# Convolution and SoLU layer: y's transposes and copies issued from a list, each behind a transpose of p, from tile 17 on

## Chip, cores and metric

The kernel runs on one core of a Trainium2 chip. The metric is the device time of one execution in microseconds; lower is better. Before the change three runs took 1172.75, 1173.3 and 1176.29 us, median 1173.3 us.

## What is computed

x has 8 sequences of 4160 positions with 192 features. The first step is a causal convolution over 7 positions with softmax weights for each of 8 heads; the second is a feed-forward layer of width 1024 with the SoLU activation and a layer norm. Cut to what matters:

```python
def _attn_ref(x, weight):                      # weight: 8 heads x 7 taps
    ...
    w = w / (np.sum(w, axis=-1, keepdims=True) + 1e-09)
    ...
    out = np.einsum('hk,bskhg->bshg', w, x_unf)
    return out.reshape(B, S, D).astype(np.float32)

def _moe_ref(x, w_in, w_out, g_ln):            # 33280 x 192, 192 x 1024, 1024 x 192
    h = x @ w_in
    h_max = np.max(h, axis=-1, keepdims=True)
    e = np.exp(h - h_max)
    sm = e / (np.sum(e, axis=-1, keepdims=True) + 1e-09)
    solu = h * sm
    mu = np.mean(solu, axis=-1, keepdims=True)
    var = np.mean((solu - mu) ** 2, axis=-1, keepdims=True)
    ln = (solu - mu) / np.sqrt(var + 1e-06) * g_ln
    return (ln @ w_out).astype(np.float32)
```

## The kernel before

The 33280 rows are 260 **tiles** of 128 rows (index i). The convolution works on **chunks**: 17 pieces of a sequence, from chunk 2 on half a sequence (2080 rows) each, so 16 or 17 tiles. The first tiles of chunks 2 to 16 are 16, 32, 48, 65, 81, 97, 113, 130, 146, 162, 178, 195, 211, 227 and 243.

**A chunk's way.** `load` (L139) brings x into buffers xr, four pieces a chunk. `sum_squares` (L174) takes the largest magnitude of half a piece on VectorE (L181, into xa); from all of them `scale_steps` makes the chunk's scale (L203 and after). GpSimd splits x into two float16 parts, xs (L236, L240, L243; `halve_steps`). `product` (L258) convolves on TensorE (L281, into pc); ScalarE writes y's upper part (`upper`, L313) and VectorE its lower (`lower`, L322) into y16. A chunk's y16 has two parts, the first ten windows of 112 rows and the other nine, each with three blocks of 128 columns (0: upper, 2: lower, 1: the rest of both). `turn` (L351) transposes one block of one part into yT by a DMA on SyncE's queue (L352), in the order of blocks 1, 0, 2; `double` (L361) copies half of block 1 to y2 (L365). `open` (L327) gets yT and y2 for a chunk and copies the rows that the chunk before left over.

**A tile's way.** `emit_rows` (L730) multiplies blocks 0, 0, 2, 1 of yT with w_in in eight matmuls (L736, into ph), in this order; `emit_third` (L756) adds the lower part of w_in with half arrays (L759) from yT's block 1 or from y2. VectorE takes the maximum (`emit_max`, L790), ScalarE the exponential (L797), VectorE the product (L807), ScalarE the upper half p (L815), GpSimd the lower half (`emit_lo`, L827), and behind it SyncE issues the transpose of p into pT (L829). Five tiles later `emit_out` (L831) multiplies pT with w_out (L843, into po); VectorE adds it up into raw (`emit_evac`, L850), later the row's factor is applied (L917, L921) and two tiles' rows are stored (L930).

**What sets the order.** Everything is in the order in which the program is written. From tile 8 on `three_steps` (L1276) issues a **triplet** of tiles a, b, c; its first tile i is 8, 11, 14, and so on. All DMAs stand in SyncE's one queue, in order, and a transpose of p waits there for its p. `chores` (L964) spreads a chunk's loads, convolutions, transposes (`"turn"`), copies (`"double"`) and sums over the tiles of the chunk before it, or of one two or three chunks before. In a triplet with i ≥ 16 (`start` is false), x's loads come at the beginning; opening and transposes that are due come at the end, behind the transpose of p of c (`openings`, L1334); copies that are due wait in `doubles` until the next triplet, behind the transpose of p of its a. Triplets with i < 16 are ordered otherwise.

Of the kernel before, what the change touches and what calls it, by code (L numbers as in the profile page):

```python
# [19 lines left out]
def kernel(  # L20
# [346 lines left out]
    chunks = [Chunk(ch) for ch in range(NCH)]  # L367
# [184 lines left out]
    for e, bank in enumerate(banks):  # L552
        for q in range(2 * per):
# [4 lines left out]
                start=q == 0, stop=q == 2 * per - 1,  # L558
# [267 lines left out]
    def emit_lo(t, eng):  # L826
        eng.tensor_tensor(t.p16[:, :, 1, :], t.halves, t.p16[:, :, 0, :], ALU.subtract)  # L827
        t.pT = sp.tile([P, 2 * NFC, P], F16, name=f"pT_{t.i}", tag="pT", bufs=4)
        nc.sync.dma_start_transpose(t.pT, t.p16.rearrange("p n a f -> p (n a f)"))  # L829
# [113 lines left out]
    tiles, lefts, left = [], [], 0  # L943
# [153 lines left out]

    PAIRED = FIRST // P
    assert spans[0][2] == PAIRED * P and PAIRED == 8 and (NT - PAIRED) % 3 == 0
    early, doubles, squares, late = [], [], [], []  # L1100

    def prepare(i):
        t = tiles[i]
# [15 lines left out]
    def numerators(t):  # L1119
        emit_mul(t)  # L1120
        emit_hi(t)
# [142 lines left out]
    def others(ts):  # L1264

        work = {}
        for q in ts:
            for what, items in chores(q.ch, q.k, q.n).items():
                work.setdefault(what, []).extend(items)
        return work  # L1270

    def loads(work):
        for c, j in work.get("load", []):
            c.load(j)

    def three_steps(i):  # L1276
# [4 lines left out]
        work = others(ts)  # L1281
# [13 lines left out]
        urgent = i == PAIRED + 3  # L1295

        start = i < 2 * PAIRED
        if not start:
            loads(work)
        got = {}  # L1300

        def add(n):
            for c, h in added[n]:
                sum_up(c, h, i + 2)
# [16 lines left out]
        def at(n):  # L1321
            return [q for q in got.get(n, []) if q]

        def uppers(n):
            for k, pc, hg in at(n):
                if not k.scaled and k.exact:
                    run_chain(20)
                k.upper(pc, *hg)

        def lowers(n):  # L1330
            for k, pc, hg in at(n):
                k.lower(pc, *hg)

        def openings():  # L1334
            for k in work.get("open", []):
                k.open(lefts[k.ch], chunks[k.ch - 1])
            for k, piece in work.get("turn", []):
                k.turn(*piece)
# [40 lines left out]
            doubles.clear()  # L1379
        numerators(a)  # L1380
        emit_lo(a, pool)
        if i == PAIRED:
            uppers(2)
            late[:] = after
# [17 lines left out]
        emit_square(a)  # L1402
        numerators(b)
        emit_lo(b, pool)
        if not start:
            lowers(2)
        for f in rest:
            f()
# [27 lines left out]
        if urgent:  # L1436
            for k, q in work["double"]:
                k.double(*q)
        else:
            openings()  # L1440
            doubles.extend(work.get("double", []))
        if i == NT - 6:
            ready(b)
        queue.run(3.8 if i < 20 else 2.0)
# [2 lines left out]
    def ready(t):  # L1447
        emit_z(t)
        emit_root(t)
# [58 lines left out]
    for i in range(PAIRED, NT - 3, 3):  # L1508
        three_steps(i)
# [28 lines left out]
```

## Time and profile before

| | |
|---|---|
| median of three runs | 1173.3 us (1172.75 to 1176.29) |
| the profiled execution, whole | 1174.77 us |
| its span, first to last instruction | 1173.1 us |
| TensorE matmuls busy | 97% of the span |
| DMA on SyncE's queue | 1.0 busy share of 16 engines in most of 40 slices |
| granted TensorE clock | 1.00 in every slice |

How to read the profile: PE is TensorE's matmuls, PEld its weight loads, DVE VectorE, ACT ScalarE, POOL GpSimd. SPq is SyncE, which only issues DMAs; a row's duration there is the time until SyncE goes on, not that of the transfer. Names stand without buffer numbers, y for both y16 and y2, p for p16. A timeline row has start, duration (both us), engine, line, operation, out<-in, the shapes and the count of rows merged into it; in square brackets the time that the engine stood idle ahead of it and what ended that. In the view of one tile a row has the shortest, median and longest duration in ns, and the first and last start. A row of the waits has who waited, for whom, the sum in us, how often, and the longest.

### The profile page before, as it was taken

How to read it: one execution, taken by the hardware profiler on the slowest of the kernel's cores; microseconds unless marked ns; L12 is line 12 of the kernel's file. 1: busy time of each engine (PE TensorE's matmuls, PEld its weight loads, DVE VectorE, ACT ScalarE, POOL GpSimd, SP SyncE). 2: the span in 40 equal slices, each digit the busy share in tenths (PEclk: the TensorE clock that was granted, in tenths of full speed). 3: DMA queues.
4: the chain of work that ended last, by engine and by line, in shares of the span. 5: the costliest groups of instructions: out<-in, count | busy, mean ns of one | idle time of the engine just before them, and what ended most of it. 6: DMA issues, size and time to landing. Idle time of an engine off the chain costs nothing.

```text
span 1173.1 us, 22240 instructions
## 1 busy us (share of the span) xinstructions
PE 1135.2 (97%) x7678; PEld 687.5 (59%) x7678; DVE 1019.3 (87%) x2057; ACT 998.8 (85%) x1773; POOL 877.6 (75%) x683
## 2 busy tenths in 40 slices
PE   5899999999999999999999999999999999999997
PEld 4455555555565665656556665665666566566555
DVE  8888798888989898898889989888898998788787
ACT  7998888887888888888888888888888889888885
POOL 1746788887878588787867888588788858855664
PEclk9999999999999999999999999999999999999999
DMA  7999999999999999999999999999999999999987
GB/s 220 180 185 174 181 206 204 206 185 201 197 206 205 184 191 193 222 182 200 206 196 192 195 215 202 186 204 204 209 196 193 202 193 173 178 165 194 181 161 175
DMA packets 727295, 226.95 MB, mean 193 GB/s; under 512 B 651518, under 2 KB 725774, under 8 KB 727182
## 3 DMA queue, kind: packets, MB, share of 16 engines
q1 hardware_dynamic: 727182, 225.53, 100.0%
q8 instruction: 60, 0.98, 0.3%
q14 instruction: 53, 0.43, 0.1%
HBM read 33.00 MB, written 25.56 MB: 50 GB/s over the span
## 4 chain that ended last, share of the span: by engine, by line
PE 70%; POOL 8%; DVE 6%; DMA 5%; issue 5%; ACT 4%; SPq 2%; POOLq 0%; DVEq 0%; ACTq 0%
PE po L843 32%; PE ph L736 29%; POOL p L827 5%; PE pc L281 5%; PE ph L759 4%; DMA pT<-p 4%; DVE ph L790 2%; DVE e L807 1%; ACT p L815 1%; ACT e L797 1%; ACT sq L819 1%; POOL xs L243 1%; DMA raw_in<-in_moe_w_in_dram 1%; POOL xr L240 1%; SPq L829 1%
## 5 line engine op out<-in xcount | busy, mean ns | idle before, releaser
L827 POOL TENSOR_TENSOR p<-e,p 128x1024 f16<-128x1024 f32 x259 | 552.8, 2138 | 237.6 <-ACT p L815 237.6
L843 PE MATMUL po<-ohl,pT 128*128 128x384 f16 (+1 forms) x4200 | 540.9, 285 | 15.3 <-DMA pT<-p 10.8
L843 PEld LDWEIGHTS <-pT 128*128 128x128 f16 x4200 | 379.3, 98 | 180.5 <-DMA pT<-p 15.5
L736 PE MATMUL ph<-whi,yT 128*128 128x512 f16 x1548 | 419.1, 380 | 5.5 <-DVE e L807 4.7
L790 DVE TENSOR_SCALAR_CACHE_REDUCE ph<-ph,cv 128x1024 f32<-128x1024 f32 x248 | 319.1, 1288 | 80.0 <-PE ph L759 63.0
L797 ACT ACTIVATE e<-ph,sm 128x1024 f32<-128x1024 f32 x260 | 289.5, 1113 | 103.8 <-DVE ph L790 96.1
L807 DVE SCALAR_TENSOR_TENSOR e<-ph,cv,e 128x1024 f32<-128x1024 f32 x248 | 317.0, 1278 | 22.2 <-ACT e L797 21.9
L736 PEld LDWEIGHTS <-yT 128*128 128x128 f16 x2064 | 192.4, 98 | 234.7 <-issue 35.6
L815 ACT CAST p<-e 128x1024 f16<-128x1024 f32 x260 | 269.9, 1038 | 31.7 <-DVE e L807 31.1
L819 ACT ACTIVATE sq<-e 128x1024 f32<-128x1024 f32 x260 | 273.5, 1052 | 0.1
L850 DVE TENSOR_REDUCE raw<-po 128x192 f32<-128x384 f32 x255 | 140.5, 551 | 16.9 <-PE po L843 16.6
L736 PE MATMUL ph<-wlo,yT 128*128 128x512 f16 x516 | 153.5, 379 | 0.0
L243 POOL TENSOR_TENSOR xs<-xr,xs 128x960 f16<-128x960 f32 (+1 forms) x56 | 107.6, 1922 | 1.4
L313 ACT ACTIVATE y<-pc 112x432 f16<-112x432 f32 (+5 forms) x140 | 62.9, 470 | 20.3 <-PE pc L281 11.7
L281 PE MATMUL pc<-xs,taps_hi 128*112 128x240 f16 (+1 forms) x448 | 73.0, 261 | 1.5 <-DVE xm L203 1.5
L759 PE MATMUL ph<-wlo,yT 64*128 64x512 f16 x269 | 74.0, 380 | 0.0
L322 DVE SCALAR_TENSOR_TENSOR y<-pc,y 112x432 f16<-112x432 f32 (+5 forms) x140 | 72.1, 532 | 0.7 <-ACT y L313 0.7
L181 DVE TENSOR_REDUCE xa<-xr 128x1 f32<-128x384 f32 x112 | 66.6, 617 | 3.5 <-DMA xr<-in_x_dram 3.5
L759 PE MATMUL ph<-wlo,y 64*128 64x512 f16 x251 | 68.6, 380 | 0.0
L281 PEld LDWEIGHTS <-taps_hi 128*112 128x112 f16 x448 | 52.4, 130 | 18.2 <-DVE xm L203 1.8
L240 POOL TENSOR_SCALAR xr<-xr,s 128x960 f32<-128x960 f32 (+1 forms) x56 | 57.6, 1029 | 3.0
L281 PE MATMUL pc<-xs,taps_lo 128*112 128x240 f16 (+1 forms) x224 | 58.5, 261 | 0.0
(145 smaller groups left out, 779.1 us busy)
## 6 DMA issues: line engine op xcount, KB each, us to landing
out_dram<-raw SPq DMA_DIRECT2D x127, 192.0 KB, 3.0
xr<-in_x_dram SPq DMA_DIRECT2D x41, 480.0 KB, 5.2
xr<-in_x_dram SPq DMA_DIRECT2D x22, 384.0 KB, 4.2
pT<-p SPq DMA_TRANSPOSE x260, 4.7
y<-yT SPq DMA_DIRECT2D x15, 140.0 KB, 3.1
y<-yT SPq DMA_DIRECT2D x15, 126.0 KB, 2.9
yT<-y SPq DMA_TRANSPOSE x102, 3.7
raw_out<-in_moe_w_out_dram SPq DMA_DIRECT2D x1, 1536.0 KB
```

The costliest lines, as they stand in the source:

```text
L243: (2.1 * size + 0.2, lambda: pool.tensor_tensor(xl, r, h, ALU.subtract)),
L281: nc.tensor.matmul(o, tp[:, h + j, :], r, start=q == 0, stop=q == len(ops) - 1)
L736: nc.tensor.matmul(bank, lhs, w[:, r, n * 512 : (n + 1) * 512], start=start and j == 0, stop=stop and j == len(ops) - 1,)
L759: nc.tensor.matmul(banks_of(t)[n], y[q, t.off : t.off + P], wlo[q, 1, n * 512 : (n + 1) * 512], start=start, stop=not start,)
L790: dve.tensor_scalar(t.ph, t.ph, t.cv[:, 0:1], None, ALU.mult, ALU.min, accum_out=t.bias)
L797: act.activation(t.e, t.ph, AF.Exp, bias=t.bias, scale=-1.0, accum_out=grp.z[:, g : g + 1])
L807: dve.scalar_tensor_tensor(t.e, t.ph, t.cv[:, 3:4], t.e, ALU.mult, ALU.mult, accum_out=t.grp.s1[:, t.g : t.g + 1],)
L815: act.copy(t.p16[:, :, 0, :], t.halves)
L819: act.activation(junk, t.e, AF.Square, accum_out=t.grp.s2[:, t.g : t.g + 1])
L827: eng.tensor_tensor(t.p16[:, :, 1, :], t.halves, t.p16[:, :, 0, :], ALU.subtract)
L843: nc.tensor.matmul(t.po[:, 0:n], t.pT[:, a, :], w, start=j == 0, stop=j == len(ops) - 1)
L850: dve.tensor_reduce(t.grp.raw[:, t.g, :], t.po[:, 0 : 2 * D].rearrange("p (a d) -> p d a", a=2), AX.X, ALU.add,)
```

## The change

Three edits in `three_steps`, all for triplets with i ≥ 17 (i ≥ 16 in the code; the first such triplet is 17):

- x's loads are issued behind b's transpose of p instead of at the triplet's beginning.
- Transposes of y and copies go to a list, `moves`. One entry is taken behind the transposes of p of a, of b and of c. What comes due in a triplet is put on the list at its end, behind c's own taking, so it goes out in the next triplet at the earliest.
- Ahead of each copy an empty entry is put on the list, so that a copy has one tile's distance from the transpose ahead of it. Openings stay where they were.

```diff
-    early, doubles, squares, late = [], [], [], []
+    early, doubles, squares, late, moves = [], [], [], [], []
...
         start = i < 2 * PAIRED
-        if not start:
-            loads(work)
         got = {}
+
+        def move():
+
+            for f in moves[:1]:
+                f()
+            del moves[:1]
...
         numerators(a)
         emit_lo(a, pool)
+        move()
...
         numerators(b)
         emit_lo(b, pool)
+        move()
         if not start:
+            loads(work)
             lowers(2)
...
-        else:
+        elif start:
             openings()
             doubles.extend(work.get("double", []))
+        else:
+            move()
+            for k in work.get("open", []):
+                k.open(lefts[k.ch], chunks[k.ch - 1])
+            moves.extend(lambda k=k, q=q: k.turn(*q) for k, q in work.get("turn", []))
+            for k, q in work.get("double", []):
+                moves.extend((lambda: None, lambda k=k, q=q: k.double(*q)))
```

On PE, ACT and POOL the order of instructions stays the same. On SP it changes from tile 20 on; on DVE only memsets of xr move with their loads.

SP's queue from the transpose of p of tile 19 (p_19) to that of tile 22, before (y_2_10 is the second part of chunk 2, xr_0 and xr_1 are pieces of chunk 5's x):

```order
L829 DMA_TRANSPOSE pT_1337<-p_19_1331 128x16x128
L352 DMA_TRANSPOSE yT_920<-y_2_10_912 128x9x112 x2
L151 DMA xr_0_1341<-in_x_dram 112x192
L160 DMA xr_0_1341<-in_x_dram 128x4x192
L160 DMA xr_1_1345<-in_x_dram 128x5x192
L930 DMA out_dram<-raw_534 128x2x192
L829 DMA_TRANSPOSE pT_1418<-p_20_1415 128x16x128
L930 DMA out_dram<-raw_978 128x2x192
L829 DMA_TRANSPOSE pT_1454<-p_21_1451 128x16x128
L829 DMA_TRANSPOSE pT_1513<-p_22_1508 128x16x128
```

The same place with the change:

```order
L829 DMA_TRANSPOSE pT_1337<-p_19_1331 128x16x128
L930 DMA out_dram<-raw_534 128x2x192
L829 DMA_TRANSPOSE pT_1410<-p_20_1407 128x16x128
L352 DMA_TRANSPOSE yT_920<-y_2_10_912 128x9x112
L930 DMA out_dram<-raw_978 128x2x192
L829 DMA_TRANSPOSE pT_1447<-p_21_1444 128x16x128
L352 DMA_TRANSPOSE yT_920<-y_2_10_912 128x9x112
L151 DMA xr_0_1450<-in_x_dram 112x192
L160 DMA xr_0_1450<-in_x_dram 128x4x192
L160 DMA xr_1_1454<-in_x_dram 128x5x192
L829 DMA_TRANSPOSE pT_1513<-p_22_1508 128x16x128
```

The two transposes of y that stood behind p_19 stand behind p_20 and p_21, and the loads that stood ahead of p_20 stand ahead of p_22.

DVE with the change, from tile 22's product to the next chunk's maximum of scale; this piece is the same before, and it holds the first instruction that reads the xr_0 loaded above:

```order
L807 SCALAR_TENSOR_TENSOR e_1493,s_16_999<-ph_1374,cv_715,e_1493 128x1024
L850 TENSOR_REDUCE raw_1439<-po_1521 128x192
L181 TENSOR_REDUCE xa_1576<-xr_0_1450 128x1
L790 TENSOR_SCALAR ph_1538,sm_1578<-ph_1538,cv_715 128x1024
L322 SCALAR_TENSOR_TENSOR y_3_0_1392<-pc_0_6_1547,y_3_0_1392 112x10x48
L203 TENSOR_REDUCE xm_1503<-pc_0_6_1547 128x1
```

The maximum of xr_0 (L181) stands ahead of tile 23's maximum (L790) in both; nothing moved here, the load of what it reads did.

SP's queue from p_26 to p_31, before (y_3_0 is the first part of chunk 3, whose first tile is 32; y_3 without a second number is its y2):

```order
L829 DMA_TRANSPOSE pT_1771<-p_26_1768 128x16x128
L365 DMA y_3_1693<-yT_1692 64x1120
L829 DMA_TRANSPOSE pT_1809<-p_27_1806 128x16x128
L829 DMA_TRANSPOSE pT_1852<-p_28_1848 128x16x128
L352 DMA_TRANSPOSE yT_1692<-y_3_0_1400 128x10x112 x2
L829 DMA_TRANSPOSE pT_1927<-p_29_1924 128x16x128
L930 DMA out_dram<-raw_1446 128x2x192
L829 DMA_TRANSPOSE pT_1955<-p_30_1952 128x16x128
L829 DMA_TRANSPOSE pT_2004<-p_31_1999 128x16x128
```

With the change:

```order
L829 DMA_TRANSPOSE pT_1768<-p_26_1765 128x16x128
L352 DMA_TRANSPOSE yT_1692<-y_3_0_1392 128x10x112
L829 DMA_TRANSPOSE pT_1806<-p_27_1803 128x16x128
L160 DMA xr_3_1808<-in_x_dram 128x4x192
L829 DMA_TRANSPOSE pT_1851<-p_28_1847 128x16x128
L365 DMA y_3_1693<-yT_1692 64x1120
L829 DMA_TRANSPOSE pT_1925<-p_29_1922 128x16x128
L352 DMA_TRANSPOSE yT_1692<-y_3_0_1392 128x10x112
L930 DMA out_dram<-raw_1439 128x2x192
L829 DMA_TRANSPOSE pT_1954<-p_30_1951 128x16x128
L352 DMA_TRANSPOSE yT_1692<-y_3_0_1392 128x10x112
L829 DMA_TRANSPOSE pT_2004<-p_31_1999 128x16x128
```

Block 1 moved from behind p_25 to behind p_26, block 0 from behind p_28 to behind p_29, block 2 from behind p_28 to behind p_30, and the copy from behind p_26 to behind p_28. In the same way the last transpose of the first part stands behind p_44, 60, 77, 93, 110, 126, 143, 158, 174, 191, 207, 224 and 239 for chunks 4 to 16.

## The prediction

> **What bounds the kernel now.** First the busy times on the page, then the table of waits, last the timeline at the places where TensorE waits. The page, with its lines on transposes:
>
> ```profile
> span 1173.1 us, 22240 instructions
> PE 1135.2 (97%) x7678; PEld 687.5 (59%) x7678; DVE 1019.3 (87%) x2057; ACT 998.8 (85%) x1773; POOL 877.6 (75%) x683
> ...
> pT<-p SPq DMA_TRANSPOSE x260, 4.7
> ...
> yT<-y SPq DMA_TRANSPOSE x102, 3.7
> ```
>
> TensorE is busy for 97% of the span; the others have room. The change alters no arithmetic, so it can only remove idle time of TensorE or add some. What there is to remove stands in the waits from 195 to 1150 us (weight loads first, then matmuls):
>
> ```profile
> PEld L843 <- DMA pT<-p: 10.9, 10, 2.2
> PE po L843 <- DMA pT<-p: 7.6, 8, 1.9
> ```
>
> Ten times in all, tile 33 the first and tile 177 the last, the weights of the second product wait for the transpose of p. The matmuls start 7.6 us later for it in sum (weights are otherwise loaded about 0.2 us ahead, so the weight load's wait is longer). Before 195 us there is little of this, and behind 1150 us stand the last tiles, which the change doesn't touch. **7.6 us is therefore the most that can be won there.** How such a wait comes about, at tile 33:
>
> ```profile
> 187.35 4.86 SPq L352 DMA_TRANSPOSE yT<-y  x3
> 192.26 1.39 SPq L160 DMA_DIRECT2D xr<-in_x_dram  x2
> 193.74 2.26 SPq L930 DMA_DIRECT2D out_dram<-raw  x1
> 196.11 3.58 SPq L829 DMA_TRANSPOSE pT<-p  x1
> ...
> 201.06 4.92 SPq L829 DMA_TRANSPOSE pT<-p  x2
> ...
> 194.83 2.13 POOL L827 TENSOR_TENSOR p<-e,p 128x1024 f16<-128x1024 f32 x1
> ...
> 205.99 1.09 PEld L843 LDWEIGHTS <-pT 128*128 128x128 f16 x10 [1.83 <-DMA pT<-p]
> ```
>
> SyncE issues three transposes of y, two loads and a store in one piece, and the transpose of p of tile 32 comes behind them. That of tile 33 is issued at 201.06, though its p was ready at 194.83 + 2.13 = 196.96. TensorE loses 1.83 us of its lead at 205.99.
>
> **What the change removes.** Bursts like this one are taken apart: one transpose of y between two of p, the loads behind the tile b of a triplet. I take the whole 7.6 us off; the bounds are 4 (a single transpose or the loads still stand ahead of a close one) and 8. The same number of DMAs is issued, so their sum is no term.
>
> **What it adds, at the first tile of a chunk.** A transpose of y that was found due in a triplet went out at that triplet's end. Now it goes into the list, and waits for the p of a, b or c of the next triplet, or of the one behind that. TensorE's order is unchanged, and its first tile of a chunk reads all three blocks of yT, block 2 last of the list. So the last of the three now stands behind a p that VectorE, ScalarE and GpSimd finish late, while TensorE is already at the next tiles. Chunk 3 (first tile 32) is the plainest: block 0 behind p of 29, block 2 behind p of 30, where both stood behind 28. Its place in the trace:
>
> ```profile
> 178.60 2.31 SPq L829 DMA_TRANSPOSE pT<-p  x1
> ...
> 179.06 2.15 POOL L827 TENSOR_TENSOR p<-e,p 128x1024 f16<-128x1024 f32 x1
> ...
> 179.21 0.59 PE L736 MATMUL ph<-whi,yT 128*128 128x512 f16 x2 [0.30 <-POOL xs L243]
> 179.64 0.59 PE L736 MATMUL ph<-wlo,yT 128*128 128x512 f16 x2
> 180.69 1.04 PE L736 MATMUL ph<-whi,yT 128*128 128x512 f16 x4 [0.46 <-DMA yT<-y]
> ...
> L829 SPq DMA_TRANSPOSE pT<-p x260: 1581/2284/5373, 38.8 to 1163.5; - x130
> ...
> L352 SPq DMA_TRANSPOSE yT<-y x102: 1194/1586/3012, 16.6 to 1097.6; - x102
> ```
>
> TensorE already waits 0.46 us for block 2, and begins with it at 180.69. p of 30 is ready at 179.06 + 2.15 = 181.21. From there its own transpose takes SyncE 2.3 us to issue (the median of the last rows; 1.6 at least), and block 2 lands 3.7 us later (the page): 6.0 us together. 181.2 + 6.0 = 187.2, less 180.7: **6.5 us of waiting**. Nothing covers it, since TensorE works in order and all behind it waits too.
>
> The same sum holds at chunks 8, 10 and 15, whose first tile is tile a of its triplet, with the last transpose behind tile a of the triplet just before. The end of that p, then the start of the matmuls on block 2 (the row with x4):
>
> ```profile
> 529.31 2.14 POOL L827 TENSOR_TENSOR p<-e,p 128x1024 f16<-128x1024 f32 x1 [2.41 <-ACT p L815]
> 533.92 1.03 PE L736 MATMUL ph<-whi,yT 128*128 128x512 f16 x4
> ...
> 671.62 2.14 POOL L827 TENSOR_TENSOR p<-e,p 128x1024 f16<-128x1024 f32 x1 [2.64 <-ACT p L815]
> 676.23 1.03 PE L736 MATMUL ph<-whi,yT 128*128 128x512 f16 x4
> ...
> 1018.59 2.14 POOL L827 TENSOR_TENSOR p<-e,p 128x1024 f16<-128x1024 f32 x1 [2.65 <-ACT p L815]
> 1023.20 1.03 PE L736 MATMUL ph<-whi,yT 128*128 128x512 f16 x4
> ```
>
> 531.45 + 6.0 − 533.92 = 3.5; 673.76 + 6.0 − 676.23 = 3.5; 1020.73 + 6.0 − 1023.20 = 3.5. With chunk 3 that is 17.0. At the ten other chunks from 4 on the first tile is b or c, or the p lies a triplet further back. The first (tile 48) and the last of them (tile 243):
>
> ```profile
> 242.21 2.13 POOL L827 TENSOR_TENSOR p<-e,p 128x1024 f16<-128x1024 f32 x1 [0.53 <-ACT p L815]
> 250.02 0.81 PE L736 MATMUL ph<-whi,yT 128*128 128x512 f16 x3
> ...
> 1082.87 2.14 POOL L827 TENSOR_TENSOR p<-e,p 128x1024 f16<-128x1024 f32 x1 [4.74 <-ACT p L815]
> 1090.07 1.03 PE L736 MATMUL ph<-whi,yT 128*128 128x512 f16 x4
> ```
>
> 244.34 + 6.0 − 250.02 = 0.3 and 1085.01 + 6.0 − 1090.07 = 0.9. Read in the same way the ten give 2 us together. Where two blocks go out behind two p's that follow each other closely (chunks 7, 9, 12, 14), SyncE gets to the second p about 1 to 2.5 us after it is ready, since a transpose of y (1.6) and a store stand ahead: 5 us more. I take 7; the bounds are 2 and 10. Second parts of chunks and y2's copies are read tiles later and cost nothing.
>
> **What it adds, at x's loads.** From tile 20 on xr of chunk 5 is loaded in the triplet whose successor sums it. There VectorE is waiting for that load today:
>
> ```profile
> 132.67 4.22 POOL L827 TENSOR_TENSOR p<-e,p 128x1024 f16<-128x1024 f32 x2
> ...
> 134.62 3.82 SPq L352 DMA_TRANSPOSE yT<-y  x2
> ...
> 138.48 0.58 SPq L151 DMA_DIRECT2D xr<-in_x_dram  x1
> 139.11 0.97 SPq L160 DMA_DIRECT2D xr<-in_x_dram  x2
> 140.18 0.47 SPq L930 DMA_DIRECT2D out_dram<-raw  x1
> ...
> 143.18 0.55 DVE L181 TENSOR_REDUCE xa<-xr 128x1 f32<-128x384 f32 x1 [3.52 <-DMA xr<-in_x_dram]
> ...
> 145.63 0.39 PE L281 MATMUL pc<-xs,taps_hi 128*112 128x216 f16 x2 [1.48 <-DVE xm L203]
> ```
>
> VectorE stands 3.52 us, and TensorE then waits for VectorE (1.48 us at 145.63; the maximum, L203, is queued behind that sum). The load was issued at 139.11 and landed 4.1 us later. Now p of 20 and of 21, two transposes of y and two stores go ahead of it. From 134.6: store 0.5, p 2.3, y 1.6, store 0.5, p 2.3, y 1.6, the small piece of x 0.6 give an issue at 144.0, and 144.0 + 4.1 = 148.1: **5 us later**, and TensorE with it. Bounds: 3 with the shortest issues (1.6 and 1.2), 8 if the transposes ahead are as slow as 4.45 us, which tile 20's was in the burst. For later chunks the loads begin at the chunk's first tile and the sums at its middle, some eight tiles behind, so the move costs nothing there; their memsets only change place on VectorE.
>
> **The sum.** 17.0 + 7 + 5 − 7.6 = +21.4 us. Against the profiled execution (1174.8 us, of which 1173.1 are the span and 1.7 lie around it) that is 1196; that execution is 1.5 above the median of the runs, 1173.3, so **1195 us**.
>
> **The rivals.** First, *the waits at the chunks cost less*: p may come sooner after TensorE, with VectorE and GpSimd less behind. With the fastest issues and landings, 1 us less at each chunk leaves 13 + 2, with 3 at the load and 7.6 won: +10, or 1184. Between the two lies anything. Second, *faster*: the spread transposes land in time. This needs each p to be ready earlier than today by the waits above, 6.5 and 3.5 us; then 7.6 are won, 1166. The point where it decides is a sum of new waits under 7.6, a third of what I read; the 0.46 us that chunk 3 already waits speaks against it. Third, *no change*: new and old waits cancel, or the list is empty when it counts; but the order of SyncE's instructions shows the list at work at each chunk.
>
> Fourth, *a slow array behind long waits*. At the start of the trace, sixteen matmuls of one shape take nearly twice as long as a little later:
>
> ```profile
> 16.17 3.52 PE L281 MATMUL pr<-xr,taps 128*112 128x120 f32 x16
> ...
> 26.72 1.89 PE L281 MATMUL pc<-xr,taps 128*112 128x120 f32 x16
> 30.78 0.60 PE L736 MATMUL ph<-whi,yT 128*128 128x512 f16 x2 [2.16 <-DVE e L807]
> ```
>
> 3.52 against 1.89, behind an idle start. Behind the 2.16 us at 30.78 the pace is the usual one, and no longer wait stands in the body of the trace. The new waits are longer: about 6.5 at the load (1.5 + 5), 6.5 in two pieces at tile 32, and three of 3.5. If behind each of two to five of them as much work as the wait is long (3.5 us) went at that pace, each would lose 3.5 × (1 − 1.89 / 3.52) = 1.6: 3 to 8 us, and the time is 1200. [...]
>
> **How the numbers follow.** Forecast 0.64 (1188 to 1199); slow array 0.15 (1198 to 1208); smaller waits 0.13 (1177 to 1188); no change 0.05; faster 0.03. The range is 1184 to 1208: it takes in the bounds 10 (chunks) and 8 (load) with the slow array. A measurement of this kernel tells 0.3% (3.5 us) from no change. Faster 0.03, same 0.05, slower 0.92.
>
> **What would show it.** Right: in the waits of TensorE, L736 on DMA yT<-y rises from 0.5 us to 15 or more, 6 of them at tile 32; VectorE's L181 on DMA xr waits 8 instead of 3.5; waits of L843 on DMA pT in the middle go from 7.6 to under 2. Wrong: if p of 30, 110, 143 and 224 is ready 3 us earlier in its relation to TensorE, or if matmul groups behind the waits are no slower and waits on pT come back elsewhere.

## The result and the profile after

The change takes 1212.06 us in the median of five runs (1210.53 to 1216.92), against 1173.3 before: 1.0336 times the time, with an interval of 1.0317 to 1.0356. It is slower by some 39 us; 1195 had been forecast, with 1208 as the end of the range. The profiled execution took 1212.06 us, its span is 1210.4, that is 37.3 longer than before.

The page of the changed kernel, with the span, the busy times and the granted clock in 40 slices:

```profile
span 1210.4 us, 22214 instructions
PE 1144.9 (95%) x7678; PEld 691.2 (57%) x7678; DVE 1019.2 (84%) x2057; ACT 999.0 (83%) x1773; POOL 876.7 (72%) x683
PEclk9999998999999999999999989999999999999999
```

TensorE has the same 7678 matmuls and is 9.7 us longer busy with them (1144.9 against 1135.2). Its idle time, span less busy time, goes from 37.9 to 65.5 us, which is 27.6 more. Both together are the 37.3. So the loss has two parts that are explained apart: more waiting, and slower matmuls.

The waits of the changed kernel over the whole span (who waited for whom, the sum in us, how often, the longest):

```profile
PE ph L736 <- DMA yT<-y: 24.9, 10, 4.9
PE pc L281 <- DVE xm L203: 8.2, 1, 8.2
PE po L843 <- DMA pT<-p: 7.1, 6, 2.0
PE ph L759 <- DMA y<-yT: 1.4, 1, 1.4
```

Over its whole span the kernel before had these:

```profile
PE po L843 <- DMA pT<-p: 10.8, 11, 1.9
PE ph L736 <- DMA yT<-y: 0.5, 1, 0.5
PE pc L281 <- DVE xm L203: 1.5, 1, 1.5
```

The wait for yT has grown by 24.4, the one behind x's load by 6.7, a wait for y2 is new (1.4), and that for pT has shrunk by only 3.7. The timeline of the changed kernel at x's late load, SyncE's queue first:

```profile
139.43 1.30 SPq L352 DMA_TRANSPOSE yT<-y  x1
140.82 0.55 SPq L930 DMA_DIRECT2D out_dram<-raw  x1
141.48 2.12 SPq L829 DMA_TRANSPOSE pT<-p  x1
143.65 1.60 SPq L352 DMA_TRANSPOSE yT<-y  x1
145.31 0.58 SPq L151 DMA_DIRECT2D xr<-in_x_dram  x1
145.93 0.98 SPq L160 DMA_DIRECT2D xr<-in_x_dram  x2
...
149.69 0.55 DVE L181 TENSOR_REDUCE xa<-xr 128x1 f32<-128x384 f32 x1 [10.21 <-DMA xr<-in_x_dram]
152.14 0.61 PE L281 MATMUL pc<-xs,taps_hi 128*112 128x216 f16 x2 [8.17 <-DVE xm L203]
```

The load goes out behind the transposes of p of 20 and 21 and two of y; VectorE stands 10.2 us, and TensorE 8.2 for it. The timeline at tile 32, the first of chunk 3:

```profile
186.28 2.13 POOL L827 TENSOR_TENSOR p<-e,p 128x1024 f16<-128x1024 f32 x1
...
187.61 1.36 SPq L352 DMA_TRANSPOSE yT<-y  x1
189.07 0.62 SPq L930 DMA_DIRECT2D out_dram<-raw  x1
189.78 2.04 SPq L829 DMA_TRANSPOSE pT<-p  x1
...
191.01 1.01 PE L736 MATMUL ph<-whi,yT 128*128 128x512 f16 x2 [4.89 <-DMA yT<-y]
191.81 1.06 PE L736 MATMUL ph<-wlo,yT 128*128 128x512 f16 x2
191.87 1.75 SPq L352 DMA_TRANSPOSE yT<-y  x1
...
195.75 1.89 PE L736 MATMUL ph<-whi,yT 128*128 128x512 f16 x4 [2.88 <-DMA yT<-y]
```

Here are both parts side by side. TensorE waits 4.89 us for block 0 and 2.88 for block 2. The row of GpSimd is p of 30, ready at 188.41; its transpose goes out only at 189.78, since SyncE is still busy with block 0 and a store. And what TensorE then does is slow: the groups of two take 1.01 and 1.06 us where they took 0.59 before the change, the group of four 1.89 where it took 1.04. At the first tiles of four later chunks (8, 10, 14, 15):

```profile
556.01 1.89 PE L736 MATMUL ph<-whi,yT 128*128 128x512 f16 x4 [3.11 <-DMA yT<-y]
703.91 1.89 PE L736 MATMUL ph<-whi,yT 128*128 128x512 f16 x4 [3.71 <-DMA yT<-y]
986.14 1.04 PE L736 MATMUL ph<-whi,yT 128*128 128x512 f16 x4 [1.72 <-DMA yT<-y]
1059.47 1.04 PE L736 MATMUL ph<-whi,yT 128*128 128x512 f16 x4 [3.10 <-DMA yT<-y]
```

The same 1.89 follows two of the three waits of 3 us and more, the usual 1.04 the third of them and the short one. The granted clock in the stretches around the slow places (start and end, length, then busy time and instructions of PE, PEld, DVE, ACT, POOL, then the clock, the DMAs' share and GB/s):

```profile
146.00:157.00 11.00, 4.86 (x18) 2.60 (x19) 7.13 (x17) 4.20 (x7) 0.78 (x1) 0.53 0.71 164
190.00:201.00 11.00, 7.11 (x25) 3.13 (x25) 0.92 (x1) 1.89 (x5) 4.66 (x3) 0.53 0.80 163
555.00:560.00 5.00, 3.99 (x19) 2.40 (x19) 0.12 (x1) 0.65 (x2) 2.64 (x3) 0.66 1.04 211
702.00:710.00 8.00, 6.09 (x23) 3.06 (x24) 1.76 (x3) 1.92 (x4) 2.83 (x3) 0.57 1.07 212
```

The records of the clock show 0.5 for 10.2, 10.2, 3.4 and 6.8 us in these stretches, 30.7 in all, and 1.00 elsewhere in the body. TensorE is busy for 22.05 us in them; had all of it been at half pace, half would be loss, 11.0. The 9.7 of longer busy time fits into that.

These lengths are 3, 3, 1 and 2 times 3.41 us, and the starts (146.13, 190.51, 555.73 and 702.51) lie 13, 107 and 43 times that apart, so the records of this trace can be read as a row of windows of that length. The last three at tile 32, at half clock each:

```profile
190.50:193.91 3.41, 1.86 (x4) 0.43 (x4) 0.00 (x0) 0.00 (x0) 3.41 (x3) 0.50 1.06 209
193.91:197.32 3.41, 1.57 (x4) 0.64 (x5) 0.00 (x0) 0.00 (x0) 0.75 (x1) 0.50 1.08 202
197.32:200.74 3.42, 3.42 (x16) 1.96 (x15) 0.66 (x1) 1.63 (x4) 0.00 (x0) 0.50 0.26 73
```

The window ahead of them has no matmul at all, and behind it the clock falls; the next two are busy for 1.86 and 1.57 us, and it stays low; the third is full, and behind it the clock is 1.00 again. At the other three places of this trace the clock fell behind windows with 1.26, 0.58 and 1.11 us of matmuls (from 142.72, 552.32 and 699.09), stayed low behind windows with 0.00, 0.82 and 2.01 us (from 146.13, 149.55 and 702.51), and was 1.00 again behind windows with 3.41, 3.14 and 3.41 us (from 152.96, 555.73 and 705.92). The wait of 3.10 us at 1059 is split over two windows, which are still busy for 2.29 and 1.44 us, and the clock stays at 1.00. Where between these numbers it turns, the trace does not show.

### The profile page after: what moved, and what is told of

It reads as the page before. It is cut to its first block, busy times and chain, and to the rows that moved or that the text cites. A ratio compares the mean times of both kernels' runs of the same rounds, so it can differ in the third digit from the quotient of the medians.

```text
span 1210.4 us, 22214 instructions
## 1 busy us (share of the span) xinstructions
PE 1144.9 (95%) x7678; PEld 691.2 (57%) x7678; DVE 1019.2 (84%) x2057; ACT 999.0 (83%) x1773; POOL 876.7 (72%) x683
## 4 chain that ended last, share of the span: by engine, by line
PE 55%; POOL 18%; issue 8%; DVE 7%; DMA 5%; ACT 5%; SPq 2%; POOLq 0%; ACTq 0%; DVEq 0%
PE po L843 24%; PE ph L736 23%; POOL p L827 11%; PE pc L281 4%; PE ph L759 3%; DMA yT<-y 3%; DVE ph L790 2%; POOL xs L243 2%; POOL xr L240 2%; ACT p L815 2%; SPq L829 1%; POOL t L911 1%; POOL xs L236 1%; DVE e L807 1%; ACT sq L819 1%
## 5 line engine op out<-in xcount | busy, mean ns | idle before, releaser
L843 PE MATMUL po<-ohl,pT 128*128 128x384 f16 (+1 forms) x4200 | 539.8, 285 | 10.6 <-DMA pT<-p 7.1
L843 PEld LDWEIGHTS <-pT 128*128 128x128 f16 x4200 | 379.7, 98 | 174.2 <-DMA pT<-p 10.0
L736 PE MATMUL ph<-whi,yT 128*128 128x512 f16 x1548 | 423.8, 383 | 29.7 <-DMA yT<-y 24.9
L790 DVE TENSOR_SCALAR_CACHE_REDUCE ph<-ph,cv 128x1024 f32<-128x1024 f32 x248 | 318.8, 1287 | 79.6 <-PE ph L759 61.1
L281 PE MATMUL pc<-xs,taps_hi 128*112 128x240 f16 (+1 forms) x448 | 75.0, 266 | 8.2 <-DVE xm L203 8.2
L181 DVE TENSOR_REDUCE xa<-xr 128x1 f32<-128x384 f32 x112 | 66.7, 618 | 10.2 <-DMA xr<-in_x_dram 10.2
L759 PE MATMUL ph<-wlo,yT 64*128 64x512 f16 x269 | 75.3, 385 | 0.0
L759 PE MATMUL ph<-wlo,y 64*128 64x512 f16 x251 | 70.1, 385 | 1.4 <-DMA y<-yT 1.4
L281 PEld LDWEIGHTS <-taps_hi 128*112 128x112 f16 x448 | 53.7, 133 | 25.7 <-DVE xm L203 8.5
L281 PE MATMUL pc<-xs,taps_lo 128*112 128x240 f16 (+1 forms) x224 | 59.6, 266 | 0.0
```

What stands on the lines that cost most here:

```text
L281: nc.tensor.matmul(o, tp[:, h + j, :], r, start=q == 0, stop=q == len(ops) - 1)
L736: nc.tensor.matmul(bank, lhs, w[:, r, n * 512 : (n + 1) * 512], start=start and j == 0, stop=stop and j == len(ops) - 1,)
L759: nc.tensor.matmul(banks_of(t)[n], y[q, t.off : t.off + P], wlo[q, 1, n * 512 : (n + 1) * 512], start=start, stop=not start,)
L790: dve.tensor_scalar(t.ph, t.ph, t.cv[:, 0:1], None, ALU.mult, ALU.min, accum_out=t.bias)
L843: nc.tensor.matmul(t.po[:, 0:n], t.pT[:, a, :], w, start=j == 0, stop=j == len(ops) - 1)
```

## Experiments

Ten kernels were run. Ratios are to the kernel before, run on the same chip in the same series.

### The two halves of the change

**e1: x's loads behind b, and nothing else.** On the kernel before:

```diff
-        if not start:
-            loads(work)
         got = {}
...
         if not start:
+            loads(work)
             lowers(2)
```

> The kernel before, with x's loads behind b's transpose of p as in the change; transposes and copies of y stay where they were. If the late load of chunk 5's x stops VectorE and TensorE (theory), the wait of TensorE for L203 grows from 1.5 to some 8 us, the clock halves behind it for one stretch and costs 2 us more, and all else stays: 1173 + 7 + 2 = 1182 us (1179 to 1185). If the loads are harmless and all of the loss is the list's (rival), 1171 to 1175.

Measured: 1177.22 us, ratio 1.0029 (1.0014 to 1.0043). The late load costs what the theory says, but something pays for it. The waits of this kernel:

```profile
PE pc L281 <- DVE xm L203: 8.1, 1, 8.1
PE po L843 <- DMA pT<-p: 3.7, 3, 2.6
PE ph L736 <- DMA yT<-y: 1.7, 2, 1.4
```

Of the 7.6 us of waits for pT in the middle only 0.9 is left. My expectation had them stay, since y's bursts are still in one piece here. So the bursts alone don't make p late; the loads ahead of a's transpose do, or the two together. TensorE's busy time is 1140.2, 5.0 above before, with the clock at 0.77 from 145 to 160, around the 8.1 us of waiting, which is 6.9 us at half clock; the mean of 0.992 stands for 2 × 0.008 × 1177 = 19 us in the whole execution.

**e2: the list, with the loads left where they were.** On the changed kernel:

```diff
         start = i < 2 * PAIRED
+        if not start:
+            loads(work)
         got = {}
...
         if not start:
-            loads(work)
             lowers(2)
```

> The change without its move of the loads: they come at the triplet's beginning as before, while transposes and copies of y go through the list. Theory: the waits at the first tiles of chunks stay (about 24 us on yT), with the half clock at three places (some 7.7 us), and the waits at tile 23 and its half clock (about 8 us) are gone: 1212 - 8 = 1204 us (1200 to 1207). Rival, in which the late load sets off the rest: 1185 or less.

Measured: 1207.3 us, ratio 1.0282 (1.0261 to 1.0303), 0.3 above what was expected. The list is what costs, and the load adds some 5 us to it. One thing had been missed. At tile 25, where the second part of chunk 2 is first read, this kernel's timeline has

```profile
146.73 0.60 PE L736 MATMUL ph<-whi,yT 128*128 128x512 f16 x2 [0.65 <-DMA yT<-y]
151.38 1.89 PE L736 MATMUL ph<-whi,yT 128*128 128x512 f16 x4 [3.61 <-DMA yT<-y]
```

4.3 us for a second part that I had put at nothing. In the changed kernel the 8.2 us behind the load stand ahead of it and cover it. Another thing shows in this trace: of the waits for pT in the middle only 0.3 us is left, although x's loads are where they were before the change.

### What in the list costs

**e5: due blocks are put on the list ahead of c's taking, not behind it.** On the changed kernel; every block goes out one tile earlier:

```diff
         else:
-            move()
             for k in work.get("open", []):
                 k.open(lefts[k.ch], chunks[k.ch - 1])
             moves.extend(lambda k=k, q=q: k.turn(*q) for k, q in work.get("turn", []))
+            move()
```

> The change with one thing turned round: what comes due is put on the list ahead of c's taking, so the first entry goes out behind c as before the change, and all others come one tile earlier. If the one tile of delay of the last block makes the waits at first tiles (theory), some 2.5 us are left at tile 32 and next to nothing elsewhere, 4 of 25 us; the late load stays (+6, and 2 of slow array), and of the waits for pT 1 to 3 stay: 1180 us (1177 to 1185). If taking the bursts apart is what costs, by SyncE's queue itself (rival), 1195 or more.

Measured: 1182.46 us, ratio 1.0065 (1.0049 to 1.0081), as expected. The waits of this kernel:

```profile
PE pc L281 <- DVE xm L203: 7.9, 1, 7.9
PE ph L736 <- DMA yT<-y: 5.5, 2, 2.8
PE po L843 <- DMA pT<-p: 2.8, 4, 1.9
```

The waits at the first tiles go from 24.9 to 5.5, all of it at tile 32. One tile of distance in the list is worth 30 of the 39 us. This shows the step of the prediction that ties the last blocks to a p that is finished while TensorE is already at the chunk's first tile: move them one p forward, and the wait is gone at all chunks but one.

**e8: no empty entry ahead of a copy.** On the changed kernel:

```diff
-                moves.extend((lambda: None, lambda k=k, q=q: k.double(*q)))
+                moves.append(lambda k=k, q=q: k.double(*q))
```

> The change without the empty entry ahead of a copy, so each copy to y2 comes one tile earlier. If the late copies cost (theory: GpSimd stands 5.4 us at L339 for one, TensorE 1.4 us at L759 for another, and the late p behind the first makes waits for pT of 1.1 and 2.0 us), 3 to 4 us go: 1208 us (1206 to 1210). If those waits have other causes (rival), 1212.

Measured: 1207.77 us, ratio 1.0274 (1.0255 to 1.0294), below the changed kernel's interval. The wait of L759 for y2 is gone, and the waits for pT shrink from 7.1 to 4.5. The copy to y2 is also read by GpSimd (L339). The changed kernel's timeline has

```profile
234.83 0.26 POOL L339 COPY y<-y 64x96 f16<-64x96 f16 x1 [5.39 <-DMA y<-yT]
...
248.66 2.13 PE L843 MATMUL po<-ohl,pT 128*128 128x384 f16 x16 [1.13 <-DMA pT<-p]
...
263.30 0.91 PE L843 MATMUL po<-ohl,pT 128*128 128x384 f16 x6 [1.99 <-DMA pT<-p]
```

GpSimd, which also makes the lower half of p, stands 5.39 us for y2, and two waits for pT follow within 30 us. Without the empty entry GpSimd stands 3.7 us, and in the middle 0.9 us of waits for pT is left of 3.8. So y2's later copies seem to take back part of what the change won at pT. How they do it is not shown: e2 has the same copies behind the same empty entry, GpSimd stands 4.4 us for one, and only 0.3 us of these waits is left there. Two executions of the changed kernel differ too, with 3.8 us in the trace above and 2.9 in that of e10.

### Where the old waits for pT came from

**e6: the kernel before, with the loads behind b from tile 23 on**, so that the one load that is needed early stays:

```diff
-        if not start:
+        if not start and i < 23:
             loads(work)
...
+        if i >= 23:
+            loads(work)
         if not start:
             lowers(2)
```

> The kernel before with x's loads behind b from tile 23 on; up to tile 22, and all of y's transposes and copies, as before. If the loads ahead of a's transpose of p were what made it late (theory, from the waits for pT that went away in the run with the loads alone), the ten waits go and nothing comes in their place: 1168 us (1166 to 1170). If they went away there because everything stood still for 8 us at tile 23 and the other engines caught up (rival), they come back: 1173 to 1175.

Measured: 1169.48 us, ratio 0.9958 (0.9942 to 0.9974). The waits of this kernel:

```profile
PE po L843 <- DMA pT<-p: 3.1, 3, 2.6
```

Two of these three are at the last tiles and one, of 0.3 us, in the middle, where there were 7.6, and y's bursts are still there. In its queue at the place that the prediction shows:

```profile
186.40 4.79 SPq L352 DMA_TRANSPOSE yT<-y  x3
191.29 0.72 SPq L930 DMA_DIRECT2D out_dram<-raw  x1
192.12 3.15 SPq L829 DMA_TRANSPOSE pT<-p  x1
```

The three transposes of y go out in one piece as before, but the transpose of p follows 5.7 us behind the burst's start and not 8.8, since the loads come later. The step "bursts like this one are taken apart" had the right place, and moving one member of the burst, the loads, is enough. Whether taking y's transposes apart would have been enough too, no run shows cleanly: e2 does that with the loads in place and has as little left, 0.3 us, but beside 28.5 us of waits for yT, in which the other engines can catch up.

**e4 and e7: y's first parts as before, the second parts and their copies through the list**, taken one tile earlier as in e5. e4 has the loads behind b from tile 32 on, e7 the loads from 23 on and the list from chunk 3 on. The core of the edit in e4; e7 has `q[1] == 0 or i < 23` as the first condition:

```diff
+            for k, q in work.get("turn", []):
+                if q[1] == 0:
+                    k.turn(*q)
+                else:
+                    moves.append(lambda k=k, q=q: k.turn(*q))
+            move()
+            for k, q in work.get("double", []):
+                if q[0] == 0:
+                    doubles.append((k, q))
+                else:
+                    moves.extend((lambda: None, lambda k=k, q=q: k.double(*q)))
```

> A version that keeps only what does not touch the first tile of a chunk: first parts of y and their copies where they were; second parts through the list, which is filled before c's taking, so that the first goes out behind c as before and the rest behind the next tiles; the loads as before up to tile 31 and behind b from tile 32 on. If the bursts caused the ten waits for pT (theory), 4 to 7.6 us of them go, no wait for yT comes, the clock stays at 1.0: 1166 to 1169 us. If those waits come from a late p and not from the bursts (rival), 1173.

> The loads behind b from tile 23 on, and second parts of y from chunk 3 on through the list, the first of them behind c; first parts and all up to tile 22 as before. If the second parts' bursts still make waits when the loads are out of the way, 1 to 2 us below the run with the loads alone, 1166 to 1168; if the loads were all of it, the same as that run.

Measured: e4 1169.57 us, ratio 0.996 (0.9946 to 0.9974); e7 1169.85, ratio 0.996 (0.9945 to 0.9975). e4 is 0.6 above its range, e7 where its rival had it, and both are e6 within the error. Taking the bursts of second parts apart adds nothing that can be measured to the move of the loads.

### Slow matmuls behind long waits

**e3: the changed kernel, with matmuls that compute nothing put into the four longest waits.** At tile 23 they add zeros to ph; ahead of tiles 32, 113 and 146 what they write is overwritten by the tile's first matmuls.

```diff
+    def fill(t, n, lhs=whi[:, 0, 0:P], alone=True):
+
+        for j in range(n):
+            nc.tensor.matmul(
+                banks_of(t)[j % 2], lhs, wlo[:, 0, 0:512],
+                start=alone, stop=alone,
+            )
...
         a.ph = pair(0, f"ph_{a.i}")
+        fill(a, {32: 20, 113: 14, 146: 14}.get(a.i, 0))
...
+            if i == 23:
+                fill(c, 28, nil, False)
```

> The change, with matmuls that compute nothing put into TensorE's order where it waits: 28 of 128x512 (6.0 us) at tile 23, 20 (4.3 us) ahead of tile 32, 14 (3.0 us) ahead of tiles 113 and 146. If idle time halves the clock (theory), the clock stays at 1.0 at these places, the real matmuls are some 9.7 us less busy, and the time falls to about 1203 us (1200 to 1207), since the fillers lie in waits. If the slow pace comes from something else, such as transfers or memory (rival), the clock halves all the same and the time stays at 1212 or rises by what of the 16.4 us of fillers does not fit.

Measured: 1211.1 us, ratio 1.0313 (1.0297 to 1.033). Neither side is right. Where a wait is filled the clock does what the theory says; in this kernel's timeline and window (its line numbers are ten or so higher):

```profile
144.53 6.21 PE L777 MATMUL ph<-wlo,nil 128*128 128x512 f16 x28
...
152.71 0.39 PE L281 MATMUL pc<-xs,taps_hi 128*112 128x216 f16 x2 [1.97 <-DVE xm L203]
...
156.14 2.04 PE L854 MATMUL po<-ohl,pT 128*128 128x384 f16 x15 [0.95 <-DVE s L112]
```

```profile
146.00:157.00 11.00, 8.09 (x43) 3.98 (x42) 6.57 (x17) 3.64 (x6) 0.22 (x1) 1.00 0.78 172
```

With a busy array the clock is 1.00 where it was 0.53, and the two matmuls of L281 take 0.39 us instead of 0.61. So at this place it is the idle time that halves the clock. But the time hardly falls. The larger reason is that the clock is still at half elsewhere: the mean of 0.996 stands for 2 × 0.004 × 1208 = 10 us in this execution, 3.5 of them behind the second wait at tile 32, which is not filled (0.84 from 190 to 201). Without the fillers TensorE is busy for 1141.4 us, which is 3.5 below the changed kernel and not 9.7. The smaller one is seen behind tile 23: TensorE reaches the next product with w_out (L843) sooner, and waits 0.95 us there for VectorE (L112), which has stood 10 us itself. That wait had vanished in the changed kernel, where slow matmuls covered it.

**e9 and e10: fewer of them, and the changed kernel once more beside it.** In e9 the numbers are 24 at tile 23 and 14, 10, 12, 10 ahead of tiles 32, 113, 146, 227, so that they end inside the waits; e10 is the changed kernel itself.

```diff
-        fill(a, {32: 20, 113: 14, 146: 14}.get(a.i, 0))
+        fill(a, {32: 14, 113: 10, 146: 12, 227: 10}.get(a.i, 0))
...
-                fill(c, 28, nil, False)
+                fill(c, 24, nil, False)
```

> As the run with fillers, but each shorter than its wait, so that none can cost time: 24 matmuls (5.2 us) at tile 23, 14 (3.0 us) at tile 32, 10, 12 and 10 ahead of tiles 113, 146 and 227. Compared with the change run again beside it. If a microsecond at half clock costs some 0.4 us in the end (theory, from the repeated runs of the change, 1210.5 us at 27 us of half clock and 1216.9 at 41), the half clock falls from 32 to 10 us and the time by 8 to 10, to 1203. If what the slow matmuls lose is taken from the next waits (rival, from the first run with fillers), the time falls by 1 to 3 us only, to 1210.

> The change unaltered, on the same chip as the short fillers, for comparison with them: 1212 us with some 32 us at half clock, by both theories.

Measured: e9 1209.18 us, ratio 1.0308 (1.0285 to 1.0332); e10 1214.91, ratio 1.035 (1.0327 to 1.0372). The views of the granted clock by core, e9's first, then e10's:

```profile
core 0: 1207.4 us, clock 0.994
```

```profile
core 0: 1212.0 us, clock 0.986
```

A mean clock of 0.994 is 2 × 0.006 × 1207 = 14 us at half clock, 0.986 is 34. So 20 us less at half clock make 5.7 us in the medians, 0.3 us for each; that lies between the 8 to 10 of the one side and the 1 to 3 of the other, and the intervals of the two ratios just touch, so the price is rough. The profiled executions agree: without its fillers TensorE is busy 6.0 us less in e9 than in e10 (1141.4 and 1147.4), the rest of the span, waits and fillers, is 1.4 longer, and the span is 4.6 shorter.

The record has a second way to the price. The runs of one kernel differ in their time at half clock. In the eleven kernels measured after the change, 59 runs in all, a straight line through each kernel's own runs rises by 0.34 us for each us at half clock (95%: 0.27 to 0.41). At that price the changed kernel's 31 us are worth 10 of its 39, which agrees with the 9.7 us of longer busy time.

## Why the prediction was wrong

The sum by its own terms, each with what the profiles show (us):

| term | predicted | measured |
|---|---|---|
| first tiles of chunks 3, 8, 10, 15 | 17.0 | 17.2 (7.8 + 3.1 + 3.7 + 3.1, less the 0.5 that chunk 3 waited before) |
| the other chunks from 4 on | 7 | 7.2 on yT, and 1.4 on y2 at chunk 9 |
| x's load | 5 | 6.7, less 0.95 of a wait on VectorE (L112) that the slow matmuls behind it cover |
| waits for pT won | −7.6 | −3.8 in the middle (7.6 to 3.8) |
| slower matmuls | not in the sum | 9.7 |
| **sum** | **21.4** | **37.4**, against 37.3 of the spans |

**The step that failed is the slow array.** The prediction set it beside the sum, as a rival with a chance of 0.15 and a price of 3 to 8 us, "two to five" waits at 1.6 each. It happened, in four places, and it cost 9.7. The number of places was right; the length was not. I had let half pace last for as much work as the wait is long, 3.5 us. Around the two longest waits the clock stayed at half for 10.2 us, a part of which is the wait itself, and 4.9 to 7.1 us of matmuls fell into each of the two stretches. I had also read the 2.16 us at 30.78 as harmless, from one execution. e7, whose order is the same up to there, has 8 tenths of the clock in the slice from 29 to 59 us, where the page before has 9, and of the 17 runs of the kernel before beside e1 eight have a mean clock of 0.995 to 0.997, which is 7 to 12 us at half clock. Behind the long waits the half clock varied too: it lasted 10.2 us behind tile 23's in the changed kernel's trace and 6.8 in e10's (0.53 and 0.69 from 146 to 157), and of the waits of 3.1 us, that at 556 halved the clock and that at 1059 did not. With 9.7 in the sum the forecast would have been 1205; of the rest up to 1212, 4 us are the next step's, 2 lie at the load and y2, and 1 comes from the profiled execution before, which was above its median while that after was not.

**The second step is "I take the whole 7.6 us off".** Half of it came, 3.8. The profile showed the late p rightly, and e6 shows that moving the loads is enough: the waits fall to 0.3. The changed kernel moves them too and keeps 3.8. Without the empty entry ahead of y2's copies 0.9 is left (e8), but e2, which has that entry, has 0.3, so what took the gain back stays open. The statement that "second parts of chunks and y2's copies are read tiles later and cost nothing" was wrong for y2 (1.4 us on TensorE itself, gone in e8, and with it 2.9 of the waits for pT), and for chunk 2's second part it held only because the load's wait lies ahead of it (4.3 us in e2).

**What was right.** The list's cost at the first tiles, where p is late and TensorE's order fixed: 24.4 more against 24, within 0.8 us at each of the four that the prediction works out, and e5 shows its cause. At tile 32 the larger piece was for block 0, and SyncE came to the transpose of p of 30 1.4 us after that p was ready; the sum had worked out block 2 alone and let SyncE be in time. The load: VectorE's 10.2 us were to be 8. Of the signs named, the waits for yT came (over 15, over 6 at tile 32), the load came, the drop of the waits for pT below 2 did not. The rival of smaller waits, 1184, and the faster one fall: the waits came in full.

**What stays open.** How the 9.7 us divide over the four places was not measured. The price of about 0.3 us for each us at half clock stands on one pair of kernels, whose runs scatter by 4 us or more, and on the line through the scatter, which shows that time and half clock go together and not which makes which. The three windows at half clock at tile 32 belong to two waits, 4.9 and 2.9 us with 1.9 us of work between them; e3, which fills the first of the two, has 3.5 us at half clock there (0.84 from 190 to 201), but nothing fills the second by itself. What of a burst makes p late besides the loads, and what keeps half of the waits for pT in the changed kernel, was not settled.

The version to keep is e6: two moved lines and a condition, 0.42% under the kernel before (interval 0.26 to 0.58%).

## What to carry to other kernels

When transfers are spread over an in-order queue, read for each the time at which the instruction that it now stands behind is ready, and compare it with its reader; one place in the queue was worth 30 us here. When the sum holds new waits on TensorE as long as those here (of two of 3.1 us one halved the clock), add a second term for the matmuls behind them, and put it into the sum, not beside it. When a burst makes something late, move its members one at a time before taking all of it apart: here it was enough to move the loads.

## What the runs showed of the hardware

- In the changed kernel's trace the granted clock was at half for 10.2 us around a wait of 8.2 us on TensorE, for 10.2 around two of 4.9 and 2.9 (tile 32), for 3.4 and 6.8 behind waits of 3.1 and 3.7 (at 556 and 704), and not at all behind another of 3.1 (at 1059). Around the wait of 8.3 us at tile 23 e10 has it for 6.8 us (0.69 from 146 to 157).
- In that trace the changes of the clock lie whole numbers of 3.41 us apart: it fell behind windows of that length with 0.00, 0.58, 1.11 and 1.26 us of TensorE's matmuls, not behind one with 1.44, and came back behind windows with 3.14 and 3.41.
- Matmuls without use in a wait held the clock at 1.00 in e3 (from 146 to 157; 0.53 without them), and won 5.7 us at best (e9): matmuls 6.0 us less busy, of which 1.4 went into longer waits.
- Half clock comes without the change too. In the start-up, ahead of all that the change moves, the second of the slices in e7's row of the granted clock stands at 8 tenths, in e6's at 9:

```profile
PEclk9899999999999999999999999999999999999999
```

```profile
PEclk9999999999999999999999999999999999999999
```

  Of the nine runs of the kernel before beside e9, the five with a mean clock of 1.000 or 0.999 took 1171.8 to 1173.7 us (median 1173.1), the four with 0.997 1172.0 to 1177.0 (median 1175.6): a part of the scatter of its times goes with this.
